# First rows in three loads, and a new order of the work: a state-space convolution with a gated MLP on one core

## The chip, the core and the metric

The kernel runs on one core of one Trainium2 chip. A core has five engines that run their own instruction streams and meet at semaphores: TensorE (PE in the profile; PEld is its weight load), VectorE (DVE), ScalarE (ACT), GpSimd (POOL) and SyncE (SP). Data moves between the chip's memory (HBM) and the core's two memories (SBUF for operands, PSUM for TensorE's results) by DMA, which SP and ACT issue here. The metric is the time of one execution in microseconds, lower is better. A profile is taken of one execution; its span runs from the first to the last instruction.

## The reference, cut to what matters

Sequence length S is 2048, model width 512, MLP width 1792, everything in bf16.

```python
x = A_q
xn = layernorm(x)                                  # over the 512 columns, eps 1e-5
# A: a shifted product, then a long convolution per column
k_shift = sum over t of k_pad[:, t:t + S] * shift_k[:, 3 - t]     # 4 taps
kv = k_shift * v
y = irfft(rfft(pad(kv)) * rfft(pad(ssm_k)))[:S] + kv * ssm_D
s = xn * y
# B: gated MLP
h = gelu(xn @ w_gate) * (xn @ w_up)
g = silu(h @ w_down)
return x + s * g
```

The two Fourier transforms (of `kv` and of the filter `ssm_k`) and the inverse are done as matrix products, and the term with `ssm_D` is folded into the filter's first sample.

## The kernel before, in words

**Tiling.** The 2048 rows are 16 tiles of 128 rows; four tiles form a quarter q. For the MLP each quarter is normalized (`ln`, L824: statistics L827, aggregate L828, variance plus eps L835, power -1/2 on GpSimd L836, the norm itself L846 on DVE or L845 on ACT), transposed (`xn_transpose`, L855: through TensorE at L867 for quarters 0 and 1, by DMA at L859 for quarters 2 and 3) and multiplied with 14 column chunks of the gate and up weights (`unit`, L1130). A unit is two chains of four matmuls (`psall<-xnT,Wg` and `psall<-xnT,Wu`, all recorded at L619), gelu on ACT (L1158) and the product into HT on DVE (L1161). The first two units of quarter 0 are done in halves of 256 columns (L1149, L1151), so that the first half needs tiles 0 and 1 alone. `down` (L1164) multiplies HT with the down weights.

**The convolution.** The filter `ssm_k` comes in four pieces of 128 columns, h0 to h3. `h_transpose` (L883) transposes each piece on TensorE (L891) in two halves of four transposes and copies them to HTr (L610 on ACT, L613 on DVE). `stage1` (L916) multiplies with the Fourier matrices F0 and F1 in pairs of matmuls, copies the result out on ACT and stores it to the scratch array ZH with a DMA that ACT issues. `kshift` (L961) makes the shifted product of the keys with eight passes over 128 x 2048 elements on DVE per quarter (L978 to L986), and the same stage 1 follows for it (L925, scratch array ZK). The second stage, the products of the spectra and the inverse work on 32 x 32 pieces of the TensorE array (L1001), the last step at L1231. The end is a silu, a product with the convolution's part and a sum with x, stored row tile by row tile.

**What sets the order.** Nothing is ordered by hand in the body. Each step is registered as a numbered task with its engine, an estimated duration and what it reads and writes. `Sched.run` (L345) then walks the string `SEQ` (L27), a list of all task numbers; a `b` behind a number takes the task's second choice of engine. Every engine receives its tasks in the order of that list, so each engine's queue is in order and waits at its head. The loads from HBM are tasks as well, issued by SP in the order of the string `ORDER` (L26): `x00` and `x01` are pieces of quarter 0 of x, `h0` the filter's first piece, `w0` the first gate and up weights, `D` the vector ssm_D, `x1` quarter 1, `s0` the taps and the rows that the shift needs, `k` and `v` keys and values, `d` the down weights. `LAND` (L52) says when each load is thought to land, in nanoseconds; the planner uses it, and the constants `TAKEN` (L301) and the durations given to tasks, to place buffers in its pools (eight PSUM banks above all; at most four of them hold gate and up results). It issues nothing of its own: the semaphores that the instructions wait on are found by the tracking layer from the real buffers.

At the start TensorE multiplies zeros twelve times (`warm_up`, N_WARM), then waits for the first normalized tile. DVE, in order, does the phases of the Fourier tables, the statistics of the first tiles and the norms; ACT does two sines for the tables (L722), loads the table for gelu, and then copies the transposed tiles out of PSUM.

Of the kernel before, what the change touches and what calls it, by code (L numbers as in the profile page):

```python
# [22 lines left out]
LN_EPS = 1e-5  # L23
TURN = 8192
N_WARM = 12
ORDER = "x00 h0 x01 w0 D0 h1 w1 x1 h2 h3 s0 k0 w2 k1 k2 w3 d0 d1 k3 v2 v3 v0 v1 x2 x3"  # L26
SEQ = (  # L27
# [21 lines left out]
)  # L49
NF_BANKS = 4  # L50
ISSUE = 470.0
LAND = {"x0_0": 3000, "h0": 6000, "x0_1": 7200, "wg0": 8300, "wu0": 9300, "D": 6500, "h1": 10700, "wg1": 12900, "wu1": 14600, "x1": 16000, "h2": 17400, "h3": 18700, "sk": 20000, "kh1": 21100, "kh113": 21300, "kz": 14000, "k0": 22700, "wg2": 24400, "wu2": 26100, "k1": 27600, "k2": 29100, "wg3": 30600, "wu3": 32100, "wd0": 34600, "wd1": 37200, "k3": 38500, "v2": 39800, "v3": 41100, "v0": 42400, "v1": 43700}  # L52
W_XT, W_SW, W_BK, W_BH, W_ZI, W_BI, W_ZK, W_MI, W_G1 = 1665000, 600000, 555000, 703000, 333000, 640000, 490000, 740000, 222000
NC_PAIRS = 4
SMALL = 1.15 * 262144
# [24 lines left out]
class Trk:  # L80
# [29 lines left out]
    def res(self, name, ap):  # L110
        t = ap.tensor
        tn = type(t).__name__
        if tn.startswith("SB"):
            key = "SB"
            addr = self.nc.lookup_mloc(t).addr
        else:
            assert tn.startswith("PS")
            key = "PS:" + t.name
            addr = 0
        esz = mybir.dt.size(ap.dtype)  # L120
        pairs = [list(q) for q in ap.ap]
        pst, pn = pairs[0]
        pstart = ap.offset // pst if pst else 0
        inner = ap.offset - pstart * pst
        hi = sum(st * (n - 1) for st, n in pairs[1:])
        r = Res(name, key, pstart, pstart + pn, addr + inner * esz, addr + (inner + hi + 1) * esz)
        lst = self.res_by_key.setdefault(key, [])
        for o in lst:
            if o.plo < r.phi and r.plo < o.phi and o.blo < r.bhi and r.blo < o.bhi:
                o.ovl.append(r)  # L130
                r.ovl.append(o)
        lst.append(r)
        return r
# [156 lines left out]
class Sched:  # L290
# [7 lines left out]
    SHARE_BW = 300.0  # L298
    FIRST = {"loads": 300.0, "SP": 37000.0}
    DRAIN, DRAIN2 = 121.0, 97.0  # L300
    SHARED, WAIT, TAKEN = 46000.0, 3300.0, 1400.0  # L301

    def __init__(self):
        self.tasks = []
# [91 lines left out]
def build_kernel(nc, A_q, A_k, A_v, A_shift_k, A_ssm_k, A_ssm_D, B_w_gate, B_w_up, B_w_down, out):  # L396
    with ExitStack() as es0:
# [11 lines left out]
        def new(name, shape, dt):  # L409
            h = at(name, shape, dt, place["at"])  # L410
            place["at"] += size(shape, dt)
            return h
# [4 lines left out]
        X = new("X", [128, NT, DM], BF16)  # L417
# [80 lines left out]
        S = Sched()  # L498
        res = trk.res

        def dsem(name):
            return DSem(nc.alloc_semaphore(name), name)
# [12 lines left out]
        R_X = [res(f"X{t}", X[:, t, :]) for t in range(NT)]  # L515
# [75 lines left out]
        def dma(eng, out_ap, in_ap, sem, r, w):  # L591
            trk.dma(eng, lambda e: e.dma_start(out=out_ap, in_=in_ap), sem, r=r, w=w)
# [3 lines left out]
        def load(name, out_ap, in_ap, w_res, w_buf, nbytes, ring="SP", r=(), rb=()):  # L596
            sem = dsem("d_" + name)
            last_load[0] = S.add([("loads", ISSUE)], lambda e: dma(ring, out_ap, in_ap, sem, r, w_res), r=rb, w=w_buf, nbytes=nbytes, land=float(LAND[name]))

# [23 lines left out]
        bX = [[B(f"X{q}_{t}") for t in range(4)] for q in range(NQ)]  # L623
# [47 lines left out]
        bwarm = B("warm")  # L671
# [4 lines left out]
        warm = B("pswarm", pF)  # L676
# [2 lines left out]
            for i in range(N_WARM):  # L679
                trk.op("PE", lambda h: mm(h, bank(warm), ZERO[:, 0:128], ZERO, True, True), r=[R_zero], w=R_bank(warm), accum=True)  # L680

        t_warm = S.add([("PE", 10 * 390.0 + (N_WARM - 10) * 220.0)], warm_up, r=[bwarm], w=[warm])
        bcq, bck, bid32 = B("cq"), B("ck"), B("id32")
        S.add([("POOL", 420.0)], lambda e: pool_q(), w=[bcq])
        S.add([("POOL", 1000.0)], lambda e: pool_k(), w=[bck])
# [65 lines left out]
        x_dr = A_q[0].rearrange("(p t) d -> p t d", t=NT)  # L751
# [24 lines left out]
            x_late.append(S.add([("SP", ISSUE)], lambda e: dma(e, args[0], args[1], sem, [], args[2]), w=args[3], nbytes=480000, after=last_load))  # L776

        def load_x0(t):
            ts = slice(2 * t, 2 * t + 2)
            load(f"x0_{t}", X[:, ts, :], x_dr[:, ts, :], R_X[ts], bX[0][ts], 262144)  # L780

        def load_w(i, rings=("SP", "SP")):
            f0, n = FC[i]
# [30 lines left out]

        for what in ORDER.split():
            if what[0] == "x" and len(what) == 3:
                load_x0(int(what[2]))
                continue
            {"k": load_k, "v": load_v, "w": load_w, "x": load_x, "d": load_wd, "h": lambda i: load_h(i, "SP"), "s": load_taps, "D": load_d}[what[0]](int(what[1:]))
# [81 lines left out]
        for k in range(KD):  # L901
# [4 lines left out]
                    r=[bHD, *[bHTr[k][0] for k in range(KD)]], w=[bFold], rr=[R_D, *R_HTr[0]], ww=R_HTr[0])  # L906
# [328 lines left out]
        for j in range(8):  # L1235
            p = p_y[j]
            ts = slice(2 * j, 2 * j + 2)
# [16 lines left out]
        for j in range(6):  # L1254
# [7 lines left out]
                  r=[b2], w=[B(f"out{j}")], nbytes=262144)  # L1262
# [12 lines left out]
def bass_recurrent_scan__ssm_conv_h3__glu_gated_geglu__prompt_kernel(  # L1275
    nc: bass.Bass,
    A_q: bass.AP,
    A_k: bass.AP,
    A_v: bass.AP,
    A_shift_k: bass.AP,  # L1280
    A_ssm_k: bass.AP,
    A_ssm_D: bass.AP,
    B_x: bass.AP,
    B_w_gate: bass.AP,
    B_w_up: bass.AP,
    B_w_down: bass.AP,
    out: bass.AP,
):
    build_kernel(nc, A_q, A_k, A_v, A_shift_k, A_ssm_k, A_ssm_D, B_w_gate, B_w_up, B_w_down, out)
# [28 lines left out]
```

## Time and profile before

| what | value |
|---|---|
| median of 3 runs | 194.51 us (194.4 to 194.63) |
| the execution that was profiled | 196.12 us |
| its span | 194.3 us |
| mean granted TensorE clock | 0.991 |
| PE, DVE, ACT busy | 97%, 81%, 71% |
| PE busy in 4 to 6 and in 6 to 8 us | 1.47 and 0.65 of 2 us |
| first rows of x, 256 KB | issued at 0.72 us, landed 4.12 us later |
| TensorE's first transposes | 7.35 us |
| end of TensorE's last matmul | 190.57 us |
| DMA over the span | 47.86 MB, mean 246 GB/s |

In the profile a group is a line of the kernel with its engine, operation and operands; busy time is the sum of the durations of its instructions. Matmuls overlap in the array, so a matmul of 512 columns shows some 0.38 us though the next one follows 0.216 us after it; the chain of work (the last instruction followed back to what released each step) gives the time that pieces take end to end. The granted clock is the share of full speed that TensorE was given in a stretch. The loads keep the DMA engines busy from 4 to about 40 us.

### The profile page before, as it was taken

What the parts mean: (1) busy time and instruction counts of PE and PEld (TensorE: products, weight loads), DVE (VectorE), ACT (ScalarE), POOL (GpSimd) and SP (SyncE); (2) the same over time, 40 slices, a digit from 0 to 9 for tenths busy, and PEclk for the clock granted to TensorE, in tenths of its full rate; (3) what the DMA queues carried; (4) which work ended last, traced back from release to release, by engine and by line L of the source; (5) the groups of instructions that cost most, each with busy time, mean ns of one, the idle gap of its engine ahead of it and who ended that gap; (6) DMA issues with size and microseconds to landing.
All of it is one profiled execution on the core that took longest, in us unless ns stands there. A gap on an engine that the chain in (4) does not pass through costs nothing.

```text
span 194.3 us, 3771 instructions
## 1 busy us (share of the span) xinstructions
PE 188.0 (97%) x1514; PEld 84.7 (44%) x1514; DVE 158.2 (81%) x231; ACT 137.7 (71%) x186; POOL 14.3 (7%) x32
## 2 busy tenths in 40 slices
PE   7699999999999999999999999999999999999993
PEld 2485644544434333343434433343444354444452
DVE  4878799989999798977897898899788762279784
ACT  2787899698687889895969487878767643263452
POOL 5311360000000000023000000000000000000000
PEclk9789999999999999999999999999999999999999
DMA  5999999993967997589999997841353344866056
GB/s 154 353 384 346 364 365 370 411 401 117 363 204 246 303 270 200 199 287 320 273 285 180 335 369 266 281 140 54 126 201 108 110 163 131 305 216 216 22 200 213
DMA packets 36423, 47.86 MB, mean 246 GB/s; under 512 B 7347, under 2 KB 26039, under 8 KB 36406
## 3 DMA queue, kind: packets, MB, share of 16 engines
q1 hardware_dynamic: 29878, 39.23, 62.6%
q10 hardware_dynamic: 6528, 8.39, 12.2%
q8 instruction: 12, 0.20, 0.4%
q14 instruction: 5, 0.04, 0.1%
HBM read 27.39 MB, written 14.68 MB: 217 GB/s over the span
## 4 chain that ended last, share of the span: by engine, by line
PE 94%; DMA 2%; DVE 2%; ACT 0%; issue 0%
PE psall L619 80%; PE psall L1001 6%; PE psall L891 2%; PE psall L925 2%; DMA X<-in_A_q_dram 2%; PE psall L1231 2%; PE psall L867 1%; DVE stats L827 1%; DVE G L1196 0%; DVE G L1195 0%; ACT G L1193 0%; DVE XN L846 0%; DVE mv L835 0%; DVE mv L828 0%; DVE C L701 0%
## 5 line engine op out<-in xcount | busy, mean ns | idle before, releaser
L619 PE MATMUL psall<-xnT,Wg 128*128 128x512 bf16 (+1 forms) x232 | 56.3, 376 | 0.0
L619 PE MATMUL psall<-xnT,Wu 128*128 128x512 bf16 (+1 forms) x232 | 55.7, 372 | 0.0
L619 PE MATMUL psall<-Wd,HT 128*128 128x512 bf16 (+2 forms) x238 | 52.3, 367 | 0.0
L1161 DVE TENSOR_TENSOR HT<-psall,GE 128x512 bf16<-128x512 f32 x54 | 36.5, 687 | 18.8 <-PE psall L619 17.5
L1158 ACT ACTIVATE GE<-psall 128x512 bf16<-128x512 f32 x54 | 31.3, 600 | 9.1 <-PE psall L619 8.1
L619 PEld LDWEIGHTS psall<-Wd,HT 128*128 128x128 bf16 x238 | 21.9, 98 | 27.1 <-issue 3.8
L619 PEld LDWEIGHTS psall<-xnT,Wg 128*128 128x128 bf16 x232 | 22.0, 99 | 25.9 <-issue 2.2
L619 PEld LDWEIGHTS psall<-xnT,Wu 128*128 128x128 bf16 x232 | 21.4, 98 | 25.7 <-issue 2.6
L610 ACT ACTIVATE BO<-psall 128x1024 bf16<-128x1024 f32 x18 | 17.9, 1022 | 12.0 <-PE psall L1231 6.5
L1104 DVE TENSOR_TENSOR HSW<-KB,HSW 128x2048 bf16<-128x2048 bf16 x16 | 19.1, 1218 | 1.8 <-ACT KB L610 1.7
L610 ACT ACTIVATE HSW<-psall 128x1024 bf16<-128x1024 f32 x16 | 15.5, 1026 | 2.8 <-PE psall L1001 2.8
L1185 ACT ACTIVATE G<-psall 128x512 bf16<-128x512 f32 x12 | 7.2, 596 | 12.4 <-PE psall L619 12.4
L984 DVE TENSOR_TENSOR KAC<-KAC,KTM 128x2048 bf16<-128x2048 bf16 x12 | 14.6, 1220 | 0.2
L982 DVE TENSOR_TENSOR KTM<-KK,SKB 128x2048 bf16<-128x2048 bf16 x12 | 14.6, 1219 | 0.1
L610 ACT ACTIVATE KB<-psall 128x1024 bf16<-128x1024 f32 x11 | 10.8, 1022 | 4.3 <-PE psall L1001 4.3
L610 ACT ACTIVATE AST<-psall 128x1024 bf16<-128x1024 f32 x12 | 12.2, 1020 | 1.1 <-PE psall L925 0.7
L836 POOL TENSOR_TENSOR mv<-mv,NHALF 128x1 f32<-128x1 f32 (+1 forms) x7 | 6.8, 970 | 69.2 <-DVE mv L835 69.2
L827 DVE BATCH_NORM_STATS2 stats<-X 128x6 f32<-128x512 bf16 x16 | 10.4, 678 | 1.7 <-DMA X<-in_A_q_dram 1.7
L1104 DVE TENSOR_TENSOR KB<-KB,HSW 128x2048 bf16<-128x2048 bf16 x8 | 9.7, 1218 | 0.0
L610 ACT ACTIVATE XN<-psall 128x1024 bf16<-128x1024 f32 x8 | 8.1, 1020 | 1.5 <-PE psall L619 1.3
L619 PE MATMUL psall<-HTr,F 128*128 128x512 bf16 x32 | 8.7, 379 | 0.0
L613 DVE CAST BO<-psall 128x1024 bf16<-128x1024 f32 x5 | 6.1, 1223 | 2.6 <-PE psall L1001 2.6
(83 smaller groups left out, 162.3 us busy)
## 6 DMA issues: line engine op xcount, KB each, us to landing
BH<-ZH SPq DMA_DIRECT2D x8, 512.0 KB, 5.0
HSW<-HSW SPq DMA_DIRECT2D x16, 256.0 KB, 2.8
BK<-ZK SPq DMA_DIRECT2D x8, 512.0 KB, 6.0
ZI<-BO ACTq DMA_DIRECT2D x16, 256.0 KB, 3.4
BI<-ZI SPq DMA_DIRECT2D x8, 512.0 KB, 4.6
ZK<-AST SPq DMA_DIRECT2D x6, 512.0 KB, 3.2
Hn<-in_A_ssm_k_dram SPq DMA_DIRECT2D x4, 512.0 KB, 7.4
KK<-in_A_k_dram SPq DMA_DIRECT2D x4, 512.0 KB, 12.0
```

The lines of the kernel that those rows point to most:

```text
L610: return h.activation(o, i, ACTF.Copy, scale=scale)
L613: return h.tensor_copy(o, i)
L619: return h.matmul(o, lhsT=l, rhs=r, start=st, stop=sp)
L827: t_stats[t] = op([("DVE", 670.0)], lambda e, h, t=t: h.bn_stats(stats[:, t, :], X[:, t, :]), r=[bX[q][t % 4]], w=[bst[t]], rr=[R_X[t]], w ...
L836: t_pw = op([("POOL", 850.0 if q else 600.0)], lambda e, hd, ts=ts, n=n: hd.tensor_tensor(mv[:, ts, 3:4], mv[:, ts, 2:3], NHALF[:, 0:n, :] ...
L982: op([("DVE", dur)], lambda e, h, j=j, m=m: h.tensor_tensor(KTM[:, m.slot, :, :], kk(j), sk(j), ALU.mult), r=need + [bSKB[j], a], w=[m], r ...
L984: op([("DVE", dur)], lambda e, h, m=m: h.tensor_tensor(KAC[:, a.slot, :, :], KAC[:, a.slot, :, :], KTM[:, m.slot, :, :], ALU.add), r=[m], ...
L1001: trk.op("PE", lambda h: h.matmul(ps(s, i)[b, :], lhsT=wt(col)[a, :], rhs=data(col)[a, :], start=n < 16, stop=n >= len(todo) - 16, tile_po ...
L1104: return hd.tensor_tensor(pair(KB, *(2 * DM * z for z in slots())) if to else x, k, x, ALU.mult)
L1158: op([("ACT", act(512))], lambda e, h: h.activation(GE[:, g.slot, :], bank(pg), ACTF.Gelu_apprx_tanh), r=[pg], w=[g], rr=lambda: R_bank(pg ...
L1161: op([("DVE", dve(512, 1))], lambda e, h: h.tensor_tensor(HT[:, q % 2, m, :], bank(pu), GE[:, g.slot, :], ALU.mult), r=[pu, g], w=[bHT[q][m]],
L1185: op([("ACT", act(n))], lambda e, h, g=g, pc=pc: h.activation(g, pc(), ACTF.Tanh, scale=0.5), r=[p], w=[bt], rr=lambda p=p: R_bank(p), ww= ...
```

## The change

The first quarter of x is loaded in three pieces, tile 0, tile 1, and tiles 2 and 3, in place of two pairs; tile 1 goes ahead of the filter's first piece, tiles 2 and 3 stay behind it. One load more makes one task more, so the numbers of the later tasks rise by one. `SEQ` is a new list: the order of the tasks differs on TensorE, DVE, ACT, GpSimd and SP, from the first transposes to the last stores. `LAND` has new values for every load. Two estimates for the planner are changed: what a store takes from the loads, and the time of the warm-up.

Some of what the new order moves: tile 0 is normalized first (before: tile 1). The first half-width chains are done as gate, gate, up, up. Two transposes of the filter's second piece stand ahead of the transposes of x tiles 2 and 3, and DVE, not ACT, copies one half of that piece. The first full-width unit is chunk 2 (before: chunk 4). Ahead of the first transposes of the filter's third piece stand eight half-width chains, three full-width chains and three stage-1 pairs in the old order; in the new one six, two and three. On DVE the second quarter's first key product (L978) stands after four passes of the first quarter, before the pass that ends its second tap. The first store to ZH is piece 3 (before: piece 7). In the tail, the last inverse pair (L1231) stands later among the matmuls with the down weights.

```diff
-ORDER = "x00 h0 x01 w0 D0 h1 w1 x1 h2 h3 s0 k0 w2 k1 k2 w3 d0 d1 k3 v2 v3 v0 v1 x2 x3"
+ORDER = "x00 x01 h0 x02 w0 D0 h1 w1 x1 h2 h3 s0 k0 w2 k1 k2 w3 d0 d1 k3 v2 v3 v0 v1 x2 x3"
 SEQ = (
...
-    "87 74 75 71 72 48 86 82 83 49 91 90 341 69 70 79 80 84 349 81 135 13 50 343 350 51 89 93 342 88 92b 137 351 352 14 52 54 344 53 55 345 346 353 "
...
+    "0 1 2 10 7 3 11 16 17 66 8 4 67 74 6 68 69 77 5 75 76 87 9 12 91 18 49 78 79 88 19 72 73 92 70 83 50 52 20 350 352 71 80 21 22 342 344 351 343 "
+    "13 23 54 51 84 85 90 94 81 82 89 53 56b 93b 55 125 126 14 345 24 358 360 346 354 356 25 105 106 26 353 370 110 111 372 15 432 428 27 58 430 426 "
...
-LAND = {"x0_0": 3000, "h0": 6000, "x0_1": 7200, "wg0": 8300, "wu0": 9300, "D": 6500, "h1": 10700, "wg1": 12900, "wu1": 14600, "x1": 16000, "h2": 17400, "h3": 18700, "sk": 20000, "kh1": 21100, "kh113": 21300, "kz": 14000, "k0": 22700, "wg2": 24400, "wu2": 26100, "k1": 27600, "k2": 29100, "wg3": 30600, "wu3": 32100, "wd0": 34600, "wd1": 37200, "k3": 38500, "v2": 39800, "v3": 41100, "v0": 42400, "v1": 43700}
+LAND = {"h2": 15400, "h3": 16700, "sk": 18600, "kh1": 19700, "kh113": 19900, "kz": 10600, "k0": 21100, "wg2": 22600, "wu2": 25000, "k1": 26600, "k2": 27900, "wg3": 29200, "wu3": 30500, "wd0": 32700, "wd1": 34900, "k3": 36100, "v2": 37400, "v3": 38700, "v0": 39900, "v1": 41200, "x0_0": 2950, "x0_1": 3700, "D": 6000, "h0": 6200, "x0_2": 6900, "wg0": 7800, "wu0": 8700, "h1": 10000, "wg1": 11500, "wu1": 13000, "x1": 14300}
...
-    SHARED, WAIT, TAKEN = 46000.0, 3300.0, 1400.0
+    SHARED, WAIT, TAKEN = 46000.0, 3300.0, 1600.0
...
-        t_warm = S.add([("PE", 10 * 390.0 + (N_WARM - 10) * 220.0)], warm_up, r=[bwarm], w=[warm])
+        t_warm = S.add([("PE", 7 * 427.0 + (N_WARM - 7) * 217.0)], warm_up, r=[bwarm], w=[warm])
...
         def load_x0(t):
-            ts = slice(2 * t, 2 * t + 2)
-            load(f"x0_{t}", X[:, ts, :], x_dr[:, ts, :], R_X[ts], bX[0][ts], 262144)
+            ts = slice(*((0, 1), (1, 2), (2, 4))[t])
+            load(f"x0_{t}", X[:, ts, :], x_dr[:, ts, :], R_X[ts], bX[0][ts], 131072 * (ts.stop - ts.start))
```

39 rows, old and new, of the table SEQ are left out of this document.

## The prediction

> **What bounds the kernel now.** I read the busy shares first, then the chain that ended last in order of time, then TensorE's waits, then short stretches of the opening with the granted clock, then the landings of the loads. TensorE is busy for 97% of the span, so the question is where the other 3% lies.
>
> ```profile
> PE 188.0 (97%) x1514; PEld 84.7 (44%) x1514; DVE 158.2 (81%) x231; ACT 137.7 (71%) x186; POOL 14.3 (7%) x32
> ```
>
> The chain in order of time shows that from 7.35 to 190.57 us every piece is a matmul or transpose of TensorE, without a break. Before it stands the path of the first rows: their load, statistics, normalization.
>
> ```profile
> 0.72 4.12 DMA X<-in_A_q_dram
> 4.86 0.69 DVE stats L827
> 6.97 0.33 DVE XN L846
> 7.35 0.40 PE psall L867 x4
> 9.91 1.96 PE psall L619 x12
> 11.87 0.22 PE psall L867 x4
> 182.55 8.02 PE psall L619 x43
> 190.59 0.50 ACT G L1193
> ```
>
> Read the two L867 lines against each other: the same four transposes take 0.40 us at 7.35 and 0.22 us at 11.87. The stretches of the opening say why (columns: PE busy, PEld, DVE, ACT, POOL, granted clock, DMA share, GB/s):
>
> ```profile
> 4.00:6.00 2.00, 1.47 (x6) 0.44 (x4) 1.10 (x5) 0.28 (x1) 0.00 (x0) 1.00 0.96 348
> 6.00:8.00 2.00, 0.65 (x7) 0.66 (x8) 1.48 (x5) 1.98 (x4) 1.24 (x2) 0.92 1.13 361
> 8.00:10.00 2.00, 2.00 (x13) 1.64 (x13) 1.88 (x6) 1.60 (x5) 0.55 (x1) 0.50 1.04 365
> 10.00:12.00 2.00, 2.00 (x17) 1.60 (x16) 1.49 (x4) 1.79 (x3) 0.65 (x1) 0.72 1.11 360
> 7.35 0.40 PE L867 MATMUL psall<-ident,XN 128*128 128x128 bf16 x4 [1.88 <-DVE XN L846]
> ```
>
> TensorE stands idle 1.88 us between the end of its warm-up (5.47) and the first transposes, and then has half its clock from about 7.7 to 11.1 (0.50 for 8 to 10, 0.72 for 10 to 12, full afterwards). So the opening costs twice: a late start, and 3.4 us at half clock, which is 1.7 us of work. From 7.35 on TensorE needs 190.57 - 7.35 - 1.7 = 181.5 us at full clock, and the tail behind it (last silu, two products, store) is 194.3 - 190.57 = 3.7 us.
>
> **The change part by part.** The execution that was profiled took 196.12 us: 194.3 span and 1.8 around it. The timed runs have a median of 194.51, 1.6 less. I subtract my gain from both; that the 1.6 might itself be part of the gap is a rival below.
>
> *Constants.* The estimated cost of the warm-up, the table of landings and the 1600 for 1400 only place tasks in the planner; they issue nothing. Cost 0. The new values are this trace's landings: issue time plus time to landing gives 6.98 + 8.5 = 15.5 for the filter's third piece (15.4 in the table), 10.68 + 11.9 = 22.6 for gate weights 2 (22.6), 12.44 + 14.2 = 26.6 for keys 1 (26.6). The old table had 17.4, 24.4 and 27.6.
>
> *One more load.* SP issues one more transfer ahead of the filter's first piece, 0.4 us (row SPq X: 0.40). Every later load is issued up to 0.46 later, but from 3.5 us on the queue is full (share 0.96 to 1.13), and the bytes ahead are the same. The bounds for all later landings are 0 and +0.46; I take +0.1, because the transfers wait 5 to 14 us between issue and landing.
>
> *When tile 0 lands.* Rows 0 to 1 (256 KB) took 4.12 us. In stretches of a quarter microsecond the first bytes move at 1.75, and the rates 188, 287, 188, 74, 147, 98 GB/s make 131 KB by 2.35 and 246 KB by 3.25, 1.55 before the landing. Half the bytes with the same 1.55 land at 3.9. The bounds are 4.84 (no gain: the wait isn't about bytes) and 2.95 (the new table's figure). The second tile has the bytes of the old pair: 4.8, at most 5.3.
> [...]
>
> *From tile 0 to the first matmuls.* With rows of this trace: statistics 3.9 to 4.6 (0.69), the table's phase C 0.2, aggregate, variance 5.0, power on GpSimd 0.58 to 5.7; the norm of tile 0 stands behind tile 1's statistics on DVE and ends near 6.35 (before: 7.3). First transposes 6.4. ACT's path starts at C too: two sines, table load 1.28, gelu 0.20 ended at 8.2, now near 7.3; two copies of 0.58 follow, the second ready at 8.3. Gate weights 0 land at 7.7 to 7.8. So the first gate matmuls start at 8.4 instead of 9.91.
>
> *Then a landing binds.* In the new order TensorE reaches the transposes of the filter's third piece after 16 + 16 transposes (0.9 + 1.75), six half-width chains of 0.43, three stage-1 pairs of 0.43 and two full chains of 0.865: 8.25 us of work. (Before, 9.97 us stood ahead of them; the trace has them at 19.3, long after the landing at 15.5.) From 8.4 with 1.3 us done, at full clock and with some 0.2 for the copy of the filter's second piece behind its transposes on DVE, that point comes at 15.5 to 15.6: just at the landing. So an x tile that lands anywhere up to 3.9 gives the same end: 15.6 + (181.5 - 8.25) = 188.85 for TensorE, 1.7 earlier.
>
> *What is late next.* Gate weights 2 are wanted 7.4 us later, at 23.0, and land at 22.7. Keys 1 are wanted by DVE about 5.2 us after the first shift product, which can't start before keys 0 (21.1) instead of 23.96: 26.4 against 26.7. Gate weights 3 are wanted at 30.95 and land at 29.4, but the first ZH store (27.66 in the trace) is issued near 24.8 and shares the DMA with them; such stores moved down weights 0 by about 1.9 for two. I put 0.2 us in all; the bounds are 0 and 1.
> Each of these waits stands at the head of an in-order queue: behind keys 1 on DVE are the products that free the gate and up banks, which TensorE waits for.
>
> *Middle and tail.* Same instructions, same 36 changes between array shapes (0.1 each). The nearest margins I find: the spectrum load of the keys landed at 89.0 for a use at 91.4, and is wanted 1.1 us earlier in the order: 1.3 left. In the tail the last inverse pair ends 6.2 us before TensorE does (before 8.6); two copies of 1.02, then DVE ops of 4.5 us on the way to the last row tile: free by about TensorE's end, 0.4 before its next product. 0, bounds -0.1 and +0.5.
>
> **Sum.** -1.7 + 0.2 = -1.5: span 192.8, profiled execution 194.6, median 194.51 - 1.5 = 193.0.
>
> **The rivals.**
> *The clock halves anyway.* Then 8.4 to 11.1 does 1.35 us of work, the filter's third piece is reached at 16.9, and TensorE ends at 16.9 + 173.25 = 190.15, 0.4 earlier: 194.1. For it: it has idle gaps of 0.9 and 0.5 left before 8.4. Against it: in 4.3 to 7.7, the 3.4 us ahead of the halving, TensorE was busy 1.5 us; now it has 1.2 of warm-up and about 1.1 of transposes, 67%. [...]
> [...]
> *The split does not land sooner.* At 4.84 the path is the old one, transposes at 7.35, half clock: 194.5.
> *The timed runs have no such gap (the other side).* If the 1.6 us between 196.12 and 194.51 is this gap, TensorE ended at about 189.0 there already; the new order can't end before 188.85 because 1.7 us of work was taken from ahead of the filter's third piece, and with 0.46 later landings and 0.2 of waits it ends at 189.5: 195.0. It decides when the old opening runs without the half clock. Against it: the three runs agree within 0.23 us, while a gap that comes and goes would spread them; and part of the 1.6 may be the cost of profiling, which no row here shows.
> *A store pushes gate weights 3.* Each microsecond past 30.95 is lost; past 32.6 the change is slower. Three stores' worth of delay would be needed: 195.3.
>
> **How the numbers follow.** Forecast (192.6 to 193.5) 0.47; half clock 0.18; no earlier landing 0.09; no gap in the timed runs 0.16; store 0.10. A difference of 0.2%, 0.4 us, is about what a measurement of this kernel can tell from no change. Faster: the first two, less a little, 0.62; same: the third and a third of the fourth, 0.13; slower 0.25. Predicted 193.0. The range runs from 192.6 (full 1.7 and a little tail) to 195.0, which leaves out most of the store rival and the worst of the fourth.
>
> **What would show it.** Right: the first L867 line near 6.4 with 0.22 us instead of 0.40; granted clock 1.00 throughout 8 to 12; first L619 of xnT near 8.4; the filter's third piece transposed at 15.5 to 15.7 with TensorE waiting for that load; chain unbroken after it; TensorE's end near 189. Wrong: the first X load still at 4.8; a clock of 0.50 in 8 to 10; idle of PE behind HT products or loads after 16 us.

## The result and the profile after

The changed kernel is slower: 195.33 us (median of 11 runs, 194.82 to 195.73) against 194.44 (11 runs, 194.05 to 195.34), ratio 1.0038 with a 95% interval of 1.0022 to 1.0054. A second comparison, among the experiments, gave 195.59 against 194.09, ratio 1.0071 (1.0056 to 1.0086). The two intervals do not touch: each holds for one comparison alone. Both show the changed kernel slower; by how much, 0.4 or 0.7%, stays open. The forecast was 193.0, faster by 0.8%.

The profiled execution of the changed kernel took 194.97 us with a span of 193.1. The spans listed for the other runs go from 193.0 to 193.9. Its busy times, four rows of its chain, and the stretches of the opening:

```profile
PE 187.5 (97%) x1514; PEld 83.5 (43%) x1514; DVE 158.2 (82%) x233; ACT 136.3 (71%) x184; POOL 16.0 (8%) x32
```

```profile
4.07 6.29 DMA Hn<-in_A_ssm_k_dram
10.40 0.71 PE psall L891 x4
12.06 3.91 PE psall L619 x22
15.97 0.65 PE psall L891 x4
```

```profile
4.00:6.00 2.00, 1.99 (x11) 0.70 (x9) 1.44 (x7) 1.98 (x4) 1.24 (x2) 1.00 0.92 278
6.00:8.00 2.00, 1.42 (x12) 1.23 (x12) 1.04 (x2) 1.96 (x5) 0.00 (x0) 1.00 1.04 296
8.00:10.00 2.00, 1.79 (x16) 1.44 (x16) 1.93 (x8) 1.57 (x4) 1.03 (x2) 1.00 1.03 384
10.00:12.00 2.00, 1.73 (x19) 1.56 (x18) 1.43 (x4) 1.19 (x2) 0.25 (x1) 1.00 1.11 357
```

Much of what the prediction wanted to see is there. The granted clock reads 1.00 from 4 to 12 (the first record of this trace is its rise at 4.62). Tile 0 landed at 3.04 and tile 1 at 3.46. The first transposes start at 5.6 and the first gate matmuls at 8.21, released by gate weights 0, which landed at 8.17. And against the profiled execution of before (span 194.3) the span is 1.2 us shorter. Only the time is longer. So the execution of before that was profiled is not the one that the runs show; the first experiment tests that.

What is new are waits of TensorE for loads. The waits of TensorE in the changed kernel (us in total, times, longest; the line with Q is the start of the program):

```profile
PE psall L619 <- DVE Q L704: 1.2, 1, 1.2
PE psall L619 <- DMA Wg<-in_B_w_gate_dram: 0.8, 1, 0.8
PE psall L891 <- DMA Hn<-in_A_ssm_k_dram: 0.3, 1, 0.3
PE psall L1001 <- DMA BK<-ZK: 0.2, 1, 0.2
```

The view counts a wait from the modelled end of the last matmul. Measured as the gap between the starts of two neighbouring matmuls, less what one of them takes (0.216 us for 512 columns, 0.11 for a transpose of the filter, and 0.09 more where the array changes its shape), the waits behind the first gate matmuls are 0.43 for the filter's second piece, ending at 10.40, 0.10 for its third at 15.90, a further 0.10 at each of these (the first transpose after a wait takes 0.21) and 0.25 for a key spectrum at 89.04: 0.98 us. The expectations below name 0.35 for the third piece, 0.34 for the key spectrum and 0.2 for gate weights 2; counted over every matmul of this trace they are 0.20, 0.25 and nothing. All waits below are given in this measure, with the time at which they end, unless a line of the profile is quoted.

### The profile page after: what moved, and what is told of

It is laid out like the page before. It is cut to its first block, busy times and chain, and to the rows that moved or that the text cites. A ratio compares the mean times of both kernels' runs of the same rounds, so it can differ in the third digit from the quotient of the medians.

```text
span 193.1 us, 3774 instructions
## 1 busy us (share of the span) xinstructions
PE 187.5 (97%) x1514; PEld 83.5 (43%) x1514; DVE 158.2 (82%) x233; ACT 136.3 (71%) x184; POOL 16.0 (8%) x32
## 4 chain that ended last, share of the span: by engine, by line
PE 86%; DMA 8%; SPq 2%; ACT 1%; DVE 1%; issue 0%
PE psall L619 74%; PE psall L1001 6%; DMA BK<-ZK 4%; DMA Hn<-in_A_ssm_k_dram 3%; PE psall L925 2%; PE psall L1231 2%; PE psall L891 2%; SPq L592 2%; DMA ZK<-AST 1%; ACT AST L610 1%; PE psall L867 1%; DVE G L1196 0%; DVE G L1195 0%; ACT G L1193 0%
## 5 line engine op out<-in xcount | busy, mean ns | idle before, releaser
L619 PE MATMUL psall<-xnT,Wg 128*128 128x512 bf16 (+1 forms) x232 | 55.0, 372 | 0.8 <-DMA Wg<-in_B_w_gate_dram 0.8
L619 PE MATMUL psall<-xnT,Wu 128*128 128x512 bf16 (+1 forms) x232 | 55.7, 372 | 0.0
L619 PE MATMUL psall<-Wd,HT 128*128 128x512 bf16 (+2 forms) x238 | 53.1, 367 | 0.0
L619 PEld LDWEIGHTS psall<-xnT,Wg 128*128 128x128 bf16 x232 | 21.9, 98 | 27.3 <-issue 1.8
L619 PEld LDWEIGHTS psall<-Wd,HT 128*128 128x128 bf16 x238 | 22.0, 98 | 26.9 <-issue 2.5
L619 PEld LDWEIGHTS psall<-xnT,Wu 128*128 128x128 bf16 x232 | 21.2, 98 | 26.2 <-issue 3.3
L610 ACT ACTIVATE HSW<-psall 128x1024 bf16<-128x1024 f32 x15 | 14.8, 1020 | 4.1 <-PE psall L1001 4.1
L610 ACT ACTIVATE KB<-psall 128x1024 bf16<-128x1024 f32 x13 | 12.7, 1022 | 3.8 <-PE psall L1001 3.8
L613 DVE CAST BO<-psall 128x1024 bf16<-128x1024 f32 x6 | 7.3, 1218 | 3.2 <-PE psall L1001 2.5
L1187 DVE SCALAR_TENSOR_TENSOR G<-G,psall 128x512 bf16<-128x512 bf16 x12 | 8.1, 680 | 1.9 <-ACT G L1185 1.9
L619 PE MATMUL psall<-HTr,F 128*128 128x512 bf16 x32 | 9.2, 379 | 0.0
```

The source lines that it names most:

```text
L610: return h.activation(o, i, ACTF.Copy, scale=scale)
L613: return h.tensor_copy(o, i)
L619: return h.matmul(o, lhsT=l, rhs=r, start=st, stop=sp)
L1187: op([("DVE", dve(512, 1))], lambda e, h, g=g, pc=pc: h.scalar_tensor_tensor(out=g, in0=g, scalar=1.0, in1=pc(), op0=ALU.add, op1=ALU.mult ...
```

## The experiments

The comparisons were made on several chips, on which the kernel before had medians of 194.08 to 194.21; so the ratios to it count, and the times beside them. Where a variant's text has a line less, its line numbers are one lower (L618 for L619, and so on).

### The kernel before, once more

> The kernel before, unchanged, for the spans and clocks of its usual executions. Theory A (the profiled execution of before, 196.12 us, was not its usual one: the median execution has no idle gap and no half clock at the start): median 194.4, spans near 192.6, granted clock 0.998 to 1.0, first X load landing near 3 us and first transposes near 5.6. Theory B (the opening of before is always as in its profile, and the new order loses elsewhere): clock 0.991 and span 194.3 again in the profiled execution.

Measured: 194.09 us, ratio 0.9997 (0.9988 to 1.0005), span 192.3, 2.0 less than the profiled execution of before. Four rows of the opening of its chain, and the stretches to hold against those shown in the prediction:

```profile
0.72 3.08 DMA X<-in_A_q_dram
5.68 1.28 ACT L726
7.18 1.04 ACT xnT L610 x2
8.26 1.49 PE psall L619 x12
```

```profile
4.00:6.00 2.00, 1.63 (x6) 0.45 (x4) 1.90 (x8) 1.31 (x4) 0.58 (x1) 1.00 0.90 234
6.00:8.00 2.00, 1.70 (x16) 1.41 (x16) 1.47 (x5) 1.99 (x4) 0.66 (x1) 1.00 1.09 356
8.00:10.00 2.00, 1.81 (x19) 1.58 (x19) 1.49 (x6) 2.00 (x4) 1.20 (x2) 1.00 1.04 368
10.00:12.00 2.00, 2.00 (x21) 1.70 (x20) 2.00 (x5) 1.78 (x4) 0.00 (x0) 1.00 1.10 360
```

The first pair landed at 3.80, not 4.84. TensorE was busy 1.70 of 2 us in 6 to 8, where the profiled execution had 0.65, the clock stayed at 1.00, and the first gate matmuls started at 8.26, not 9.75 (the 9.91 of the chain counts from the modelled end of the transposes before them). They are released by ACT (two sines, the table load, then the copies of the transposed tiles), whose path begins behind the same load and the first statistics. After that TensorE has one wait, 0.12 us at 10.36, up to its last matmul, which starts at 188.89. From the first gate matmul to the last matmul it takes 180.63 us, in the profiled execution 181.15; with the start 1.49 earlier that makes the 2.0 us. Profiling itself added nothing here: this profiled execution took 194.12. In the three other profiled executions of the old order below (three loads, useless work, a shorter warm-up) the mean granted clock is 0.997, 1.0 and 1.0. And all 34 executions of the kernel before in this comparison have a mean clock of 0.997 to 1.0 and spans of 192.2 to 192.8, where the profiled one had 0.991 and 194.3. So the late start and the half clock that the change was to take away belong to one execution, the profiled one.

### The three loads alone, and the new order alone

The first variant has the three loads of the change, with the old order of tasks (numbers raised by one, the new load behind its neighbour); the second has the new order with the two loads of pairs.

```diff
-ORDER = "x00 h0 x01 w0 ...
+ORDER = "x00 x01 h0 x02 w0 ...
-            ts = slice(2 * t, 2 * t + 2)
+            ts = slice(*((0, 1), (1, 2), (2, 4))[t])
```

> The three loads alone: the old order of the tasks, with the one new load put in behind the first. Theory A with the loads as the cause (one more issue of 0.46 us on SP makes every later load land about 0.45 later, and TensorE's first gate matmuls wait for gate weights 0): 194.8 to 194.9, 0.4 over before, gate weights 0 landing near 8.2 instead of 7.7. If the loads cost nothing and the new order of the tasks is the cause: 194.4. If the earlier tile helps: 193.9 or less.

> The new order of the tasks alone: the loads in two pairs as before. Theory A with the loads as the cause of all: 194.9, 0.45 under the changed kernel. If the new order costs (the filter's third piece wanted 1.7 us of work earlier, the key spectra 1.1 us earlier): 194.9 for the part that the loads cost, and still 0.4 over before. If the loads are innocent: 195.3 as the changed kernel.

Measured: three loads with the old order 194.11, ratio 0.9997 (0.9988 to 1.0005). New order with pairs 195.13, ratio 1.0051 (1.0036 to 1.0066). The three loads cost nothing and bring nothing; the loss is in the order of the tasks alone. In the trace of the new order with pairs, the chain goes through V's load, and the waits are (DVE first, then TensorE behind it):

```profile
46.24 1.22 DVE L985 TENSOR_TENSOR V<-KAC,V 128x2048 bf16<-128x2048 bf16 x1 [2.21 <-DMA V<-in_A_v_dram]
...
49.38 1.04 PE L618 MATMUL psall<-Wd,HT 128*128 128x512 bf16 x4 [0.74 <-DVE HT L1160]
```

DVE stands 2.2 us at the head of its queue for V's piece 0; behind that product is a product into HT (L1160), and TensorE's chain with the down weights waits for it. In the kernel before DVE comes to the same product at 45.20, when V's piece 0 has been there since 44.87, and it does not wait:

```profile
45.20 1.22 DVE L986 TENSOR_TENSOR V<-KAC,V 128x2048 bf16<-128x2048 bf16 x1
```

V's later landing is not the extra load's doing: in the old order with three loads V's piece 0 landed at 44.92, in the kernel before at 44.87. For gate weights 2 that is not settled: they landed at 22.60 to 23.93 us in the four traces with two loads (mean 23.24) and at 23.23 to 24.60 in the sixteen with three (mean 23.85). In the old order a later landing cost no time.

### The filter's third piece later

In the changed kernel's list of tasks, the transposes of the filter's third piece (58, 57) and a copy (59) go behind two up chains and their products:

```diff
-"... 428 27 58 430 426 28 29 30 429 427 433 359 361 57 59 355 357 31 ..."
+"... 428 27 430 426 28 29 30 429 427 433 359 361 355 357 58 57 59 31 ..."
```

> The changed kernel with the transposes of the filter's third piece moved behind one full and one half-width up chain, 1.3 us of TensorE's work later. Theory A (TensorE waits 0.4 us for that piece and nothing takes the wait's place): 0.3 to 0.4 under the changed kernel, 194.95. Theory C (the loss arises later, where TensorE waits for the key spectra at 89 us): 195.3, with the wait at 89 us longer by what the opening gains.

Measured: 196.66, ratio 1.0127 (1.0113 to 1.0142), 1.3 us over the changed kernel where a gain was expected. A wait was removed and two larger ones came: at gate weights 2, which landed at 24.20 in this execution, and among the first matmuls with V's products, at 53.28. There TensorE waited for a product into HT on DVE, which had stood 0.83 us for V's piece 0 (landed at 46.11) some products before. (This execution, 197.03 us, was the slowest of four.)

```profile
24.24 1.04 PE L618 MATMUL psall<-xnT,Wg 128*128 128x512 bf16 x4 [1.33 <-DMA Wg<-in_B_w_gate_dram]
...
53.28 0.39 PE L924 MATMUL psall<-V,F 64*128 64x512 bf16 x1 [1.10 <-DVE HT L1160]
```

The first wait had been holding TensorE back for the next load. So the waits can't be read one by one.

### Half of the new order

Both variants have the three loads. The first takes the tasks of the new list up to the gate chain of chunk 10 (205 tasks, to about 33 us) and then what is left in the old list's order; the second the old list up to the gate chain of chunk 11 (208 tasks), and then the new.

> The new order of tasks up to the gate chain of piece 10 (about 33 us), then everything that is left in the old order. If the 1.2 us that the new order loses lies in the opening (waits for the filter's second and third pieces and for gate weights 2, 0.43, 0.35 and 0.2 us in the changed kernel's trace), this kernel has most of it: 0.7 to 1.2 us over the kernel before, and the kernel with the old head has 0 to 0.4. If it lies behind 33 us (the products with V that stand at their loads' landings, the key spectra wanted earlier), this one is within 0.4 us of the kernel before. My guess: +0.7 us.

> The old order up to the gate chain of piece 11 (about 33 us), then what is left in the new order. Loss in the opening: 0 to 0.4 us over the kernel before. Loss behind 33 us: 0.7 to 1.2 us over it, with DVE waiting for V at 45 us and TensorE for the key spectrum at 88 us in its trace. My guess: +0.5 us, since both parts have waits.

Measured: new head 196.09, ratio 1.0096 (1.0082 to 1.0110); old head 203.71, ratio 1.0486 (1.0462 to 1.0509). Both are outside what was expected, because the seams bring waits of their own: a pair of 0.47 and 0.40 us at 40.01 and 43.87 in the first, and in the second one of 3.1 us from 45.85 to 48.91 for a copy on ACT. They don't split the loss. What they do show is the opening of the new order in one more execution: in the first, 0.47 for the filter's second piece and 0.77 for gate weights 2.

### Useless work on TensorE

If the new order's waits are for transfers that come when they come, work put ahead of them should cost nothing. The first two half-width up chains, ahead of all the landings in question, are issued twice: 0.87 us on TensorE, the same output.

```diff
-                    for kd in range(KD):
+                    for kd in [*range(KD)] * (2 if nm == "u" and j1 == 2 else 1):
```

> The changed kernel with the first two half-width up chains of the first chunk issued twice: 0.87 us of useless TensorE work at about 9 us, the output the same. If the changed order loses its time because TensorE reaches loads ahead of their landings, this work falls into the waits: at most 0.3 us over the changed kernel (195.3 to 195.6). If TensorE's own chain of work is what got longer in the new order, the 0.87 us come on top in full: 196.2.

> The kernel before with the same 0.87 us of useless TensorE work at about 9 us. Its trace shows no wait of TensorE after 8.3 us, so nothing can take the work in: 0.8 to 0.9 us over the kernel before, 195.0, by either theory; if it came to less than 0.4, the old order would have hidden waits of its own and the difference between the orders would not be their waits for loads.

Measured: in the changed kernel 195.29, ratio 1.0057 (1.0045 to 1.0070); in the kernel before 194.90, ratio 1.0038 (1.0026 to 1.0051), 0.71 us over it. In the old order the work costs nearly what it takes; in the new one, nothing that shows. As the changed kernel had been timed on another chip, the pair was run once more on one:

> The changed kernel once more, unchanged, beside its own variant with useless work on one chip: the first comparison of the two went over different chips, on which the kernel before differed by 0.25 us (194.44 and 194.19). 0.4 to 0.6% over the kernel before: 194.9 to 195.3.

> The changed kernel with 0.87 us of useless TensorE work at 9 us, on the same chip as the changed kernel. If that work falls into waits for loads: 0 to 0.35 us over the changed kernel of this same call. If TensorE's own chain is longer in the new order: 0.8 us over it.

Measured: changed kernel 195.59, ratio 1.0071 (1.0056 to 1.0086); with the useless work 195.01, ratio 1.0046 (1.0029 to 1.0063). More work is at least no slower. That it is faster is not shown, the intervals touch. The waits of TensorE in this execution of the changed kernel (span 193.5, the median of the first comparison and the shortest of the six in this one) are larger than in the first:

```profile
7.98 1.05 PE L619 MATMUL psall<-xnT,Wg 128*128 128x256 bf16 x8 [0.60 <-DMA Wg<-in_B_w_gate_dram]
...
10.14 0.71 PE L891 MATMUL psall<-ident,Hn 128*128 128x128 f32 x4 [0.24 <-DMA Hn<-in_A_ssm_k_dram]
...
23.96 0.39 PE L619 MATMUL psall<-xnT,Wg 128*128 128x512 bf16 x1 [0.62 <-DMA Wg<-in_B_w_gate_dram]
```

In the kernel before, TensorE had no wait for gate weights 2, which landed at 23.93; its first chain behind that landing:

```profile
24.54 1.89 PE L619 MATMUL psall<-xnT,Wg 128*128 128x512 bf16 x8
```

Both traces of the changed kernel close the account against the kernel before (first gate matmuls 8.26, waits 0.12, last matmul started at 188.89). Here the first gate matmuls start at 7.98, 0.28 earlier; then it waits 0.50 for the filter's second piece, 0.25 for its third and 0.78 for gate weights 2 (landed at 23.91), 1.53 in all. That makes -0.28 + 1.53 - 0.12 = 1.13 later; the last matmul starts at 190.04, 1.15 later. In the first trace: -0.05 + 0.98 - 0.12 = 0.81, and 189.73, 0.84 later. So the matmuls and transposes themselves take the same time in both orders, to 0.03 us, and the difference is waiting.

A second dose, the chains three times instead of once:

> The changed kernel with the useless up chains issued three times instead of twice: 1.74 us of useless TensorE work at 9 us. The first 0.87 us cost nothing (195.29 against 195.33). If its waits for loads come to about 1.3 us in a usual execution (the 0.43, 0.35, 0.2 and 0.34 of its trace), the second 0.87 us cost 0.3 to 0.6 us: 195.6 to 195.9. If they come to less than 1, it costs nearly all: 196.1. My guess: 195.8.

Measured: 195.64, ratio 1.0071 (1.0055 to 1.0087), the ratio that the changed kernel itself had on the last chip. Even 1.74 us of useless work costs 0 to 0.6 us there, by that ratio and the first one, 1.0038. TensorE has more than 1 us there in which it can only wait. The profiled execution of this variant (195.21, the fastest of its six) has no wait of TensorE left behind the first gate matmuls: from these to the last matmul it takes 182.25 us, and the kernel before without its one wait, plus the useless work, makes 180.63 - 0.12 + 1.74 = 182.25.

### Margin given back, one load at a time

V's pieces 0 and 1 loaded ahead of 2 and 3:

```diff
-ORDER = "... k3 v2 v3 v0 v1 x2 x3"
+ORDER = "... k3 v0 v1 v2 v3 x2 x3"
```

> The changed kernel with V's pieces 0 and 1 loaded ahead of 2 and 3. In its trace DVE stood 0.95 us for piece 0 at 45.4, and in the trace of the new order with paired loads TensorE stood 0.90 us at 48.3 behind that product. If these waits are a good part of the 1.2 us, the time falls by 0.4 to 0.9 us, to 194.4 to 194.9. If the loss is in the waits of the first 24 us, it falls by 0.2 at most: 195.1 to 195.4. My guess: 194.9.

The units of chunks 9 (first use of gate weights 2) and 4 in each other's place:

```diff
-"... 34 386 102 388 ... 382 384 366 142 ... 387 37 109 389 367 ... 144 368 ..."
+"... 34 366 102 368 ... 382 384 386 142 ... 367 37 109 369 387 ... 144 388 ..."
```

> The changed kernel with the gate and up chains of chunk 9 (the first that read gate weights 2) and those of chunk 4 (weights long there) in each other's place: gate weights 2 are wanted about 1.3 us later. The wait at 22.9 to 23.4 us was 0.2 to 0.8 us in the traces of the new order. If TensorE's waits are lost for good: 0.2 to 0.6 us under the changed kernel, 194.7 to 195.1. If a wait that is removed only comes back at the next late load (V at 45 us): no change, 195.3. My guess: 195.0.

Both, and the filter's second piece (54) behind the transposes of x tiles 3 and 2 (90, 89):

```diff
-"... 23 54 51 84 85 90 94 81 82 89 53 ..."
+"... 23 51 84 85 90 94 81 82 89 54 53 ..."
```

> Both edits together, and the filter's second piece transposed behind the transposes of x tiles 2 and 3 instead of ahead of them (0.43 us of wait at 10.4 in the changed kernel's trace). If the new order only lacks margin against the loads, it comes back to the time of the kernel before or under it: 193.8 to 194.5. If it has something else that is slower (engines in the middle, stores, key spectra), it stays at 194.8 or more.

Measured: V first 195.20, ratio 1.0057 (1.0039 to 1.0076); chunks swapped 194.76, ratio 1.0037 (1.0025 to 1.0050); all three 194.61, ratio 1.0023 (1.0014 to 1.0031). V first alone is a miss: DVE did not wait for V any more (45.62 for a landing at 44.01), but TensorE had waited at 23 already, and V's margin was not what counted. With the chunks swapped, TensorE waited 0.15 us at most for gate weights 2, though they landed at 24.20, and the wait came back at V. Both profiled executions were the slowest of their variant (195.95 and 195.16, medians 195.20 and 194.76), so their waits are longer than the usual ones. One line of TensorE from the trace of V first, then one of DVE from that of the swap:

```profile
24.65 0.60 PE L619 MATMUL psall<-xnT,Wg 128*128 128x512 bf16 x2 [1.35 <-DMA Wg<-in_B_w_gate_dram]
```

```profile
46.08 1.22 DVE L985 TENSOR_TENSOR V<-KAC,V 128x2048 bf16<-128x2048 bf16 x1 [2.00 <-DMA V<-in_A_v_dram]
```

So the waits stand behind one another: whoever takes away the first meets the second. Against the two ratios of the changed kernel (1.0038 and 1.0071), V first gives back nothing to 0.3 us, the swap nothing to 0.7, and all three 0.3 to 0.9; against the first of the two ratios even that is not clear of noise, since the intervals touch. In the trace with all three edits TensorE waits for no load behind 12 us. What is left of the loss is 0.5 us.

### What is left

The first half of the filter's second piece between x tiles 3 and 2 (task 54 behind 90), and then also the third piece's first half behind an up chain (58 behind 359):

> The kernel with V first and the two chunks swapped, and the first half of the filter's second piece transposed between the transposes of x tiles 3 and 2 (not behind both). In the trace with it behind both, TensorE stood 0.29 us at 10.0 for tile 2's rows and 0.51 at 11.4 for the copy of that half on DVE, and nowhere after that; it was 0.5 us over the kernel before. If these two waits are what is left of the loss, the time is that of the kernel before, 193.9 to 194.3. If something else in the new order is slower, it stays at 194.5 or more.

> The same, and the first half of the filter's third piece transposed one up chain (0.87 us) later, behind the first full chain of up weights 1. With 0.6 us less waiting at 10 to 12 us TensorE would reach that piece at 15.3, where it lands at 15.3 to 15.9; if that wait comes up, this kernel is 0.1 to 0.4 us faster than the other, 193.7 to 194.1, and so the fastest here. If the piece's landing doesn't bind, both are the same.

Measured: 194.57, ratio 1.0021 (1.0011 to 1.0031), and 195.13, ratio 1.0051 (1.0037 to 1.0065). The first edit changes nothing: the trace has 0.34 us of waiting for x tile 3's rows at 9.97, 0.23 for the copy at 11.65, 0.10 for the third piece and 0.18 at 26.67, so what one edit frees the next arrival takes. The second is a miss of the kind seen above: a wait of 0.6 us for DVE at 51.28, at the matmuls with V's products. Does what is left still consist of waits? The useless 0.87 us in the first of the two:

> The kernel with V first, the chunks swapped and the filter's second piece in the middle, with 0.87 us of useless TensorE work at 9 us. If the 0.5 us that it still has over the kernel before is waits of the opening (0.18 and 0.35 us at 9.5 to 10, 0.23 at 11.3 in its trace), the useless work falls into them and costs 0.2 to 0.4 us: 194.8 to 195.0. If TensorE's order is slower for another reason, the 0.87 us come on top: 195.4.

Measured: 194.95, ratio 1.0033 (1.0020 to 1.0046), 0.38 us for 0.87 us of work by the medians, 0.23 by the ratios. Half of it or more falls into waits, so most of the 0.5 us are waits of the opening, by this one comparison. An order of these tasks that has none of them was not found, and whether there is one stays open.

### The old order with a shorter warm-up

```diff
-N_WARM = 12
+N_WARM = 10
```

> The three loads with the old order, and ten warm-up matmuls instead of twelve. With twelve, at half clock, the warm-up lasted to 6.5 us in the trace with three loads, and tile 1's normalized rows, ready at 5.74, waited for it; first gate matmuls at 8.29. With ten the warm-up ends at 5.65 at the latest and the first gate matmuls start at 7.8 to 7.9, at gate weights 0. The old order has slack of 0.5 to 5 us at the loads behind that, so 0.3 to 0.4 us under the kernel before: 193.8. If fewer warm-up matmuls leave the clock at half for longer, up to 1 us over it.

Measured: 194.07, ratio 0.9997 (0.9989 to 1.0006). The first gate matmuls did start at 7.79, 0.47 earlier, and the last matmul at 188.75, 0.14 earlier. Between them stand the norms of x tiles 3 and 2 on DVE: their transposes start at 9.38 and 10.23, where the kernel before had 9.58 and 10.36, and TensorE waits 0.26 us for the first and 0.18 for the second. Gate weights 0 had landed at 7.66, so an earlier tile 0 could hardly have brought more here, and the next arrivals take most of it. No version ran faster than the kernel before by what can be measured.

## Why the prediction was wrong

**The step that failed** is "The timed runs have a median of 194.51, 1.6 less. I subtract my gain from both". The gain of 1.7 was worked out from the profiled execution of before, and the 1.6 was the gap itself: the usual execution starts the first gate matmuls at 8.26 (profiled: 9.75), has full clock, and its chain leaves TensorE at 188.57 (profiled: 190.57, which is the end of TensorE's part of the chain; its last matmul started at 190.90). The changed kernel was forecast to leave it at 188.85, with a span of 192.8, and the kernel before has 192.3. So there was no gain left to subtract. That is the rival "The timed runs have no such gap", at 195.0, with a chance of 0.16; it came true. Its direction was right, that the new order can't end before the old one; its terms, 0.46 of later landings and 0.2 of waits, were in part luck, for the traces have 0.98 and 1.53 of waits in other places. The argument against it, that "a gap that comes and goes would spread" the three runs, missed that the odd execution can be the profiled one alone. Taken as a forecast of a profiled execution, its 194.6 compares with a measured 194.97.

**The second step** is the term for what is late next, "I put 0.2 us in all; the bounds are 0 and 1". TensorE's waits behind the first gate matmuls were 0.98 and 1.53 us in the two traces of the changed kernel. In the prediction's own terms: the landing of the filter's second piece has no term (0.2 is put for a copy behind it), and cost 0.53 and 0.50; its third, "just at the landing", cost 0.20 and 0.25; gate weights 2, which the 0.2 in all was for, cost nothing and 0.78; the key spectrum, given a margin of 1.3 and put at 0, cost 0.25 and nothing. Each margin was taken between two numbers of one trace: gate weights 2 wanted at 23.0 and landed at 22.7, keys 1 26.4 against 26.7. But gate weights 2 land between 22.6 and 24.6 us over the 20 traces of this study, after 23.0 in 18 of them, and the profiled execution of before had the earliest landing of all. A load wanted where it landed once was late most of the time here. V's pieces were not looked at, though the new order brings DVE to them 0.7 to 2.2 us before their landing: in its traces piece 0 lands at 45.4 to 46.2, where the old order comes at 45.1 to 45.8 for a landing at 44.7 to 44.9. In the new order four stores to ZH land ahead of V's piece 0, in the old one three; that this is why it lands later is argued from the traces, not tried.

**What held.** Constants and the extra load cost nothing, as said; the term of 0.1 for "later landings" is not seen in the time, which is unchanged with three loads and the old order. Tile 0 landed at 3.04, better than the 3.9 that was taken and near the lower bound of 2.95, so "The split does not land sooner" fell. In all traces with 128 KB the first tile landed at 2.85 to 3.04; the pair, 256 KB, landed at 3.65 to 3.80 in the usual executions and at 4.84 in the profiled one of before. First transposes (6.4 forecast) came at 5.6 and first gate matmuls (8.4) at 8.21; the third piece is met at 15.9 (15.6 forecast). The clock stayed full (1.00 from 4 to 12 us), so "The clock halves anyway" fell. "A store pushes gate weights 3" did not come up: TensorE has no wait for them in any trace of the changed kernel.

## What to carry to other kernels

A profile is one execution: before subtracting a gain from a median, see that the median's execution has what the gain removes. If profiled span and usual spans differ by about the gain, the gain is probably there already, and a second profile of the unchanged kernel costs one run. The same holds for a variant's waits: a profiled execution that is not near the median shows waits that are not the usual ones.

An order of work that reaches every load at the moment it landed once has no margin: here waits of 0.98 and 1.53 us put the last matmul 0.84 and 1.15 us later; the old order's margins were small (0.6 us at the filter's second piece, 1.6 at its third, 0.6 at gate weights 2, 0.3 at V in one trace), and they were enough. Putting useless work ahead of the suspected waits is a cheap test: the 0.87 us cost 0.71 us in the kernel before and nothing that shows in the changed one, whose traces have the waits.

## What the runs showed of the hardware

The same load of the same program landed up to 1.3 us apart in two executions (kernel before: gate weights 2 at 22.60 and 23.93, the first pair of x tiles at 4.84 and 3.80), and gate weights 2 landed 2.0 us apart over all 20 traces (22.60 to 24.60). The time of the kernel before agreed within 0.2% in the eleven executions of the first experiment (194.0 to 194.4) and within 0.7% in those of the first comparison.

The mean granted clock was 0.991 in the profiled execution of before, 0.989 in that of the variant with the old head, and 0.997 to 1.0 in the 18 others. In the first the clock rose at 4.28, fell to 0.50 at 7.70 and was back at 1.00 at 11.11 (gate matmuls of 256 columns started 0.21 us apart ahead of 11.0, up matmuls of the same size 0.11 apart behind 11.2); from the rise to the fall TensorE was busy for 1.54 of 3.42 us (45%). In the variant with the old head, it fell behind one wait; a line of TensorE, then the stretches (granted clock third from the right):

```profile
48.91 1.66 PE L618 MATMUL psall<-xnT,Wg 128*128 128x512 bf16 x4 [3.06 <-ACT XN L609]
```

```profile
46.00:48.00 2.00, 0.00 (x0) 0.00 (x0) 0.00 (x0) 0.17 (x1) 0.00 (x0) 1.00 0.74 224
48.00:50.00 2.00, 1.09 (x4) 0.36 (x4) 0.55 (x1) 2.00 (x3) 0.00 (x0) 0.80 0.02 7
50.00:52.00 2.00, 2.00 (x6) 0.66 (x5) 2.00 (x3) 1.29 (x3) 0.00 (x0) 0.50 0.41 156
52.00:54.00 2.00, 2.00 (x9) 0.89 (x8) 1.97 (x3) 1.56 (x3) 0.00 (x0) 0.85 0.59 222
```

TensorE was idle from 45.85, work began again at 48.91, and by the shares of these stretches (0.80, 0.50, 0.85) the clock was at half from about 49.2 to 52.6: 3.4 us, as in the profiled execution of before (7.70 to 11.11). Here the wait of 3.1 us was followed by 3.4 us at half clock, which is 1.7 us of work.

In the opening of the changed kernel, for which the prediction had 67%, TensorE was busy for 82% of 4.62 to 8.03, behind the first rise, and the clock reads 1.00 from 4 to 12. V first has a wait of 1.35 us for gate weights 2 and a mean clock of 0.998. What decides whether the clock falls, no run shows.
